# Loads that convert to bf16 on the GpSimd queue, and relu and cos/sin factor in one VectorE instruction per chunk and factor, in a cosformer attention and hypermixer kernel

## The chip, the cores and the metric

One core of one Trainium2 chip runs the whole kernel. The metric is the device time of one execution in microseconds (us), lower is better. "Fast" and "slow" after a time are the states that each execution was given: slow here means over 1.5% above the fastest execution of the same kernel in the same set. Ratios are computed from fast executions alone: the mean time of one kernel's fast runs over that of the other's of the same rounds, so not quite the ratio of the medians that I quote. A range in brackets after a ratio is its 95% interval.

TensorE (PE) does matmuls and transposes, VectorE (DVE) and ScalarE (ACT) elementwise work and the copies out of PSUM ("evictions"), GpSimd (POOL) a few memsets, SyncE (SP) issues transfers. PEld is TensorE's weight load.

## The reference, cut to what matters

```python
# q, k, v: (8 batches, 8 heads, 576, 64) fp32
theta = np.pi / 2.0 * pos / S
def phi(x, c, s):
    r = np.maximum(x, 0.0)
    return np.concatenate([r * c, r * s], axis=-1)
q_p, k_p = phi(q, cos_w, sin_w), phi(k, cos_w, sin_w)
kv  = einsum('bhsf,bhsd->bhfd', k_p, v);  z = sum(k_p, axis=2)
x   = einsum('bhsf,bhfd->bhsd', q_p, kv) / (einsum('bhsf,bhf->bhs', q_p, z) + 1e-06)
# heads side by side: x is (8, 576, 512); then the hypermixer
wq, wk = x @ w_q, x @ w_k
mixed  = (wq @ wk.T / 8) @ x
out    = relu(mixed) @ w_out
```

## The kernel before

The factor table and a weight cast that stands in VectorE's queue behind it:

```python
    inp = ctx.enter_context(tc.tile_pool(name="inp", bufs=2))
    outpool = ctx.enter_context(tc.tile_pool(name="outpool", bufs=4))
    ...
    nc.scalar.activation(cos_t, u_f, AF.Sin, bias=0.0, scale=1.0)     # [128, 9, 1] fp32
    nc.scalar.activation(sin_t, s_f, AF.Sin, bias=0.0, scale=coef)
    cossin = consts.tile([P, C9, 2, D], BF16)
    nc.vector.tensor_copy(cossin[:, :, 0, :], cos_t.to_broadcast([P, C9, D]))
    nc.vector.tensor_copy(cossin[:, :, 1, :], sin_t.to_broadcast([P, C9, D]))
    ...
    nc.vector.tensor_copy(wo_sb, wo_f)
```

Loads, relu and products. A batch is cut into `nsplit` pieces of head pairs (4 in the first batch, 2 later), so a "half-tile" below is one piece of q or k; it has 9 chunks of 64 columns per pair:

```python
    def attention(b, x_sb, nsplit):
        qf = inp.tile([P, NPAIR, C9 * D], FP32, name="qf")            # kf, vf alike
        rq = work.tile([P, NPAIR, C9, D], BF16, name="rq")            # rk alike
        q_p = work.tile([P, NPAIR, C9, 2, D], BF16, name="q_p")       # k_p alike
        ...
        for sp in range(nsplit):
            a, bb = sp * step, (sp + 1) * step
            csb = cossin.unsqueeze(1).to_broadcast([P, step, C9, 2, D])
            for dst, rr, pp, src in ((kf, rk, k_p, k), (vf, None, None, v), (qf, rq, q_p, q)):
                ...
                nc.sync.dma_start(dst[:, a:bb, :], s4[:, a:bb, :])
                if rr is None:
                    nc.any.tensor_copy(v_ext[:, a:bb, :, 0:D], ...)
                    nc.gpsimd.memset(v_ext[:, a:bb, :, D:D + 1], 1.0)
                else:
                    nc.any.tensor_scalar(rr[:, a:bb, :, :], dst[:, a:bb, :], 0.0, None, op0=ALU.max)
                    nc.vector.tensor_mul(pp[:, a:bb, :, :, :],
                        rr[:, a:bb, :, :].unsqueeze(3).to_broadcast([P, step, C9, 2, D]), csb)
```

TensorE's use of the products, one pair at a time, and the output block after every second batch:

```python
        for pr in range(NPAIR):
            for hh in range(2):
                for c in range(C9):
                    nc.tensor.matmul(kv_ps, k_p[p0:p0 + 64, pr, c, :, :], v_ext[...], ...)
                nc.any.tensor_copy(kv_sb[:, hh, :], kv_ps)            # high priority
                if hh == 0:
                    for c in range(C9):
                        nc.tensor.transpose(qpt_ps[:, c, :], q_p[:, pr, c, :, :], ident)
            nc.vector.tensor_copy(qpt_sb, qpt_ps...)                  # high priority
            ... # num_ps matmuls, reciprocal, x_sb
    def wout(b0, mix_sb):
        for rt in range(2 * S // P):
            ... # 4 matmuls into o_ps, a tile of tag "moe_ps_e"
            o_sb = outpool.tile([P, DM], FP32, name="o_sb")
            nc.any.tensor_copy(o_sb, o_ps)
            ... # two nc.sync.dma_start of o_sb to the output
```

## Time and profile before

| kernel before | |
|---|---|
| median of 3 runs | 202.64 us (201.63 to 207.41) |
| span of the profiled execution, granted clock | 206.3 us, 0.934 |
| TensorE, VectorE, ScalarE, GpSimd busy | 168.7, 136.7, 101.0, 2.7 us |

A line of groups reads: source line, engine, operation, output<-input, shapes, count | busy us, mean ns of one | idle time just before them, and what ended it. Two rows of the page that the prediction does not show matter later: the granted TensorE clock in tenths in 40 slices of the span, and the hardware queue that carries loads and stores (packets, MB, share of 16 DMA engines' time).

```profile
PEclk9999999999999999999755999999999999965896
...
q1 hardware_dynamic: 18912, 37.76, 58.1%
...
L136 PE MATMUL kv_ps<-v_ext,k_p 64*128 64x65 bf16 x576 | 38.5, 211 | 18.9 <-DVE k_p L123 16.3
...
L147 PE MATMUL qpt_ps<-ident,q_p 128*128 128x128 bf16 x288 | 31.8, 254 | 0.2 <-DVE qpt_sb L151 0.2
```

Nearly all of the wait of TensorE for products is one piece, 16.3 us at the start. Afterwards the nine kv matmuls and nine transposes of a pair find their inputs ready and run back to back.

### The profile page before, as it was taken

How to read it: one execution, taken by the hardware profiler on the slowest of the kernel's cores; microseconds unless marked ns; L12 is line 12 of the kernel's file. 1: busy time of each engine (PE TensorE's matmuls, PEld its weight loads, DVE VectorE, ACT ScalarE, POOL GpSimd, SP SyncE). 2: the span in 40 equal slices, each digit the busy share in tenths (PEclk: the TensorE clock that was granted, in tenths of full speed). 3: DMA queues.
4: the chain of work that ended last, by engine and by line, in shares of the span. 5: the costliest groups of instructions: out<-in, count | busy, mean ns of one | idle time of the engine just before them, and what ended most of it. 6: DMA issues, size and time to landing. Idle time of an engine off the chain costs nothing.

```text
span 206.3 us, 4215 instructions
## 1 busy us (share of the span) xinstructions
PE 168.7 (82%) x1696; PEld 102.8 (50%) x1696; DVE 136.7 (66%) x301; ACT 101.0 (49%) x190; POOL 2.7 (1%) x25
## 2 busy tenths in 40 slices
PE   0007889899789999999979999999799999778950
PEld 0006677555445534866645555766554575532420
DVE  1269667945877468978886898878989497723000
ACT  2174579063923645525834858239645434114540
POOL 2000000000000000000000000000000000000000
PEclk9999999999999999999755999999999999965896
DMA  6999999999500028789995066891003870000486
GB/s 189 381 358 332 401 391 391 389 341 327 198 0 2 0 54 201 165 257 394 394 391 216 0 153 147 189 362 72 3 0 80 204 180 2 3 0 0 105 204 149
DMA packets 20514, 39.32 MB, mean 191 GB/s; under 512 B 3088, under 2 KB 3088, under 8 KB 20496
## 3 DMA queue, kind: packets, MB, share of 16 engines
q1 hardware_dynamic: 18912, 37.76, 58.1%
q10 hardware_dynamic: 1584, 1.31, 2.0%
q8 instruction: 13, 0.21, 0.5%
q14 instruction: 5, 0.04, 0.1%
HBM read 29.62 MB, written 9.44 MB: 189 GB/s over the span
## 4 chain that ended last, share of the span: by engine, by line
PE 67%; DVE 10%; DMA 9%; ACT 7%; issue 2%; SPq 1%; POOL 0%; ACTq 0%; DVEq 0%
PE moe_ps_e L244 14%; PE kv_ps L136 12%; PE qpt_ps L147 11%; PE num_ps L159 7%; PE xT_ps L180 6%; DMA kf<-in_k_dram 6%; PE moe_ps_c L213 6%; PE moe_ps_a L191 6%; PE moe_ps_d L226 4%; DMA wq_f<-in_moe_w_q_dram 2%; DVE x_sb L168 2%; ACT mix_sb L233 2%; DVE qpt_sb L151 1%; DVE xT_sb L185 1%; DVE k_p L123 1%
## 5 line engine op out<-in xcount | busy, mean ns | idle before, releaser
L136 PE MATMUL kv_ps<-v_ext,k_p 64*128 64x65 bf16 x576 | 38.5, 211 | 18.9 <-DVE k_p L123 16.3
L136 PEld LDWEIGHTS <-k_p 64*128 64x128 bf16 x576 | 27.7, 106 | 29.1 <-DVE k_p L123 16.3
L244 PE MATMUL moe_ps_e<-wo_sb,mix_sb 128*128 128x512 bf16 x144 | 35.9, 410 | 0.4 <-ACT o_sb L252 0.3
L147 PE MATMUL qpt_ps<-ident,q_p 128*128 128x128 bf16 x288 | 31.8, 254 | 0.2 <-DVE qpt_sb L151 0.2
L168 DVE TENSOR_TENSOR x_sb<-num_ps,rec 128x320 bf16<-128x320 f32 x64 | 30.1, 482 | 0.1
L151 DVE COPY qpt_sb<-qpt_ps 128x1152 bf16<-128x1152 bf16 x32 | 24.2, 756 | 7.0 <-PE qpt_ps L147 6.6
L144 ACT CAST kv_sb<-kv_ps 128x65 bf16<-128x65 f32 x44 | 9.5, 216 | 36.4 <-PE kv_ps L136 35.7
L159 PE MATMUL num_ps<-kv_sb,qpt_sb 128*128 128x65 bf16 x320 | 24.0, 214 | 1.8 <-DVE x_sb L168 1.4
L252 ACT COPY o_sb<-moe_ps_e 128x512 f32<-128x512 f32 x31 | 18.2, 586 | 14.5 <-PE moe_ps_e L244 9.5
L244 PEld LDWEIGHTS <-mix_sb 128*128 128x128 bf16 x144 | 14.7, 104 | 19.1 <-issue 5.6
L147 PEld LDWEIGHTS <-q_p 128*128 128x128 bf16 x288 | 21.1, 113 | 4.1 <-issue 1.7
L180 PE MATMUL xT_ps<-ident,x_sb 128*128 128x128 bf16 (+1 forms) x160 | 19.5, 243 | 4.2 <-DVE x_sb L168 4.2
L121 ACT ACTIVATE rk<-kf 128x1152 bf16<-128x1152 f32 (+1 forms) x17 | 18.4, 1081 | 7.5 <-DMA kf<-in_k_dram 5.7
L123 DVE TENSOR_TENSOR k_p<-rk,cossin 128x2304 bf16<-128x2304 bf16 (+1 forms) x18 | 21.8, 1213 | 0.0
L123 DVE TENSOR_TENSOR q_p<-rq,cossin 128x2304 bf16<-128x2304 bf16 (+1 forms) x18 | 21.8, 1212 | 0.0
L159 PEld LDWEIGHTS <-qpt_sb 128*128 128x128 bf16 x320 | 16.9, 109 | 9.4 <-issue 3.1
L233 ACT ACTIVATE mix_sb<-moe_ps_d 128x64 bf16<-128x64 f32 (+1 forms) x40 | 14.7, 409 | 9.7 <-PE moe_ps_d L226 8.8
L121 ACT ACTIVATE rq<-qf 128x1152 bf16<-128x1152 f32 (+1 forms) x17 | 18.5, 1086 | 1.7 <-DMA qf<-in_q_dram 1.7
L226 PE MATMUL moe_ps_d<-wqkT_sb,kx_sb 64*128 64x512 bf16 x64 | 16.7, 341 | 2.4 <-ACT mix_sb L233 1.5
L233 DVE TENSOR_SCALAR mix_sb<-moe_ps_d 128x512 bf16<-128x512 f32 (+1 forms) x24 | 11.2, 475 | 10.0 <-PE moe_ps_d L226 9.7
L116 ACT CAST v_ext<-vf 128x1152 bf16<-128x1152 f32 (+1 forms) x16 | 17.5, 1103 | 0.0
L180 PEld LDWEIGHTS <-x_sb 128*128 128x128 bf16 (+1 forms) x160 | 12.2, 108 | 10.4 <-DVE x_sb L168 4.7
(40 smaller groups left out, 106.1 us busy)
## 6 DMA issues: line engine op xcount, KB each, us to landing
out_dram<-o_sb SPq DMA_DIRECT2D x72, 128.0 KB, 2.3
kf<-in_k_dram SPq DMA_DIRECT2D x14, 576.0 KB, 10.0
vf<-in_v_dram SPq DMA_DIRECT2D x14, 576.0 KB, 9.4
qf<-in_q_dram SPq DMA_DIRECT2D x14, 576.0 KB, 9.6
kf<-in_k_dram SPq DMA_DIRECT2D x4, 288.0 KB, 5.1
vf<-in_v_dram SPq DMA_DIRECT2D x4, 288.0 KB, 5.7
qf<-in_q_dram SPq DMA_DIRECT2D x4, 288.0 KB, 6.0
wo_f<-in_moe_w_out_dram ACTq DMA_DIRECT2D x1, 1024.0 KB, 9.9
```

The lines of the kernel that those rows point to most:

```text
L121: nc.any.tensor_scalar(rr[:, a:bb, :, :], dst[:, a:bb, :], 0.0, None, op0=ALU.max)
L123: nc.vector.tensor_mul(pp[:, a:bb, :, :, :], rr[:, a:bb, :, :].unsqueeze(3).to_broadcast([P, step, C9, 2, D]), csb)
L136: nc.tensor.matmul(kv_ps, k_p[p0:p0 + 64, pr, c, :, :], v_ext[p0:p0 + 64, pr, c, :], start=(c == 0), stop=(c == C9 - 1),)
L147: nc.tensor.transpose(qpt_ps[:, c, :], q_p[:, pr, c, :, :], ident)
L151: nc.vector.tensor_copy(qpt_sb, qpt_ps.rearrange("f c (hh pp) -> f hh c pp", hh=2))
L159: nc.tensor.matmul(num_ps[:, u, :], qpt_sb[:, hh, cb:cb + 2, :], kv_sb[:, hh, :], start=True, stop=True,)
L168: nc.vector.tensor_tensor(x_sb[:, :, h, :], num_ps[:, :, 0:D], rec.to_broadcast([P, SC, D]), op=ALU.mult,)
L180: nc.tensor.transpose(xT_ps[:, j0:j0 + npn], x_sb[p0:p0 + npn, u, 2 * hp:2 * hp + 2, :], ident[p0:p0 + npn, p0:p0 + npn],)
L226: nc.tensor.matmul(mx_ps[:, 0:nn], kx_sb[:, dmc * P:(dmc + 1) * P], wqkT_sb[0:64, n0:n0 + nn], start=True, stop=True,)
L233: nc.any.tensor_scalar(mix_sb[:, dmc, half * S + n0: half * S + n0 + nn], mx_ps[:, 0:nn], scale_moe, 0.0, op0=ALU.mult, op1=ALU.max,)
L244: nc.tensor.matmul(o_ps, mix_sb[:, dmc, rt * P:(rt + 1) * P], wo_sb[:, dmc, :], start=(dmc == 0), stop=(dmc == NDM - 1),)
L252: nc.any.tensor_copy(o_sb, o_ps)
```

## The change

The intent: halve what the loads write on chip, drop the relu pass and the broadcast table, and use an operation of a higher element rate.

```diff
-    inp = ctx.enter_context(tc.tile_pool(name="inp", bufs=2))
+    inp = ctx.enter_context(tc.tile_pool(name="inp", bufs=3))
...
-    cossin = consts.tile([P, C9, 2, D], BF16)
-    nc.vector.tensor_copy(cossin[:, :, 0, :], cos_t.to_broadcast([P, C9, D]))
-    nc.vector.tensor_copy(cossin[:, :, 1, :], sin_t.to_broadcast([P, C9, D]))
...
-        qf = inp.tile([P, NPAIR, C9 * D], FP32, name="qf")      # kf, vf alike; rq, rk go
+        qb = inp.tile([P, NPAIR, C9, D], BF16, name="qb")       # kb, vb alike
...
-                nc.sync.dma_start(dst[:, a:bb, :], s4[:, a:bb, :])
+                nc.gpsimd.dma_start(
+                    dst[:, a:bb, :, :].rearrange("p pr c d -> p pr (c d)"),
+                    s4[:, a:bb, :])
...
-                    nc.any.tensor_scalar(rr[:, a:bb, :, :], dst[:, a:bb, :],
-                                         0.0, None, op0=ALU.max)
-                    nc.vector.tensor_mul(
-                        pp[:, a:bb, :, :, :],
-                        rr[:, a:bb, :, :].unsqueeze(3).to_broadcast(
-                            [P, step, C9, 2, D]),
-                        csb)
+                    for c in range(C9):
+                        for w, tab in enumerate((cos_t, sin_t)):
+                            nc.vector.tensor_scalar(
+                                pp[:, a:bb, c, w, :], dst[:, a:bb, c, :],
+                                0.0, tab[:, c, :],
+                                op0=ALU.max, op1=ALU.mult)
```

More of the change, by code (lines that the diff above doesn't have):

```diff
@@ L96, in attention @@
     def attention(b, x_sb, nsplit):
-        qf = inp.tile([P, NPAIR, C9 * D], FP32, name="qf")
-        kf = inp.tile([P, NPAIR, C9 * D], FP32, name="kf")
-        vf = inp.tile([P, NPAIR, C9 * D], FP32, name="vf")
-        rq = work.tile([P, NPAIR, C9, D], BF16, name="rq")
-        rk = work.tile([P, NPAIR, C9, D], BF16, name="rk")
+        qb = inp.tile([P, NPAIR, C9, D], BF16, name="qb")
+        kb = inp.tile([P, NPAIR, C9, D], BF16, name="kb")
+        vb = inp.tile([P, NPAIR, C9, D], BF16, name="vb")
         q_p = work.tile([P, NPAIR, C9, 2, D], BF16, name="q_p")
@@ L108, in attention @@
             a, bb = sp * step, (sp + 1) * step
-            csb = cossin.unsqueeze(1).to_broadcast([P, step, C9, 2, D])
-            for dst, rr, pp, src in ((kf, rk, k_p, k), (vf, None, None, v),
-                                     (qf, rq, q_p, q)):
+            for dst, pp, src in ((kb, k_p, k), (vb, None, v), (qb, q_p, q)):
                 s4 = src[b].flatten().rearrange(
                     "(pr p e) -> p pr e", pr=NPAIR, p=P)
-                nc.sync.dma_start(dst[:, a:bb, :], s4[:, a:bb, :])
-                if rr is None:
+                nc.gpsimd.dma_start(
+                    dst[:, a:bb, :, :].rearrange("p pr c d -> p pr (c d)"),
+                    s4[:, a:bb, :])
+                if pp is None:
                     nc.any.tensor_copy(
-                        v_ext[:, a:bb, :, 0:D],
-                        dst[:, a:bb, :].rearrange("p pr (c d) -> p pr c d", c=C9))
+                        v_ext[:, a:bb, :, 0:D], dst[:, a:bb, :, :])
                     nc.gpsimd.memset(v_ext[:, a:bb, :, D:D + 1], 1.0)
                 else:
-                    nc.any.tensor_scalar(rr[:, a:bb, :, :], dst[:, a:bb, :],
-                                         0.0, None, op0=ALU.max)
-                    nc.vector.tensor_mul(
-                        pp[:, a:bb, :, :, :],
-                        rr[:, a:bb, :, :].unsqueeze(3).to_broadcast(
-                            [P, step, C9, 2, D]),
-                        csb)
+                    for c in range(C9):
[4 more added lines that the diff above has]
+                                op0=ALU.max, op1=ALU.mult)
         for pr in range(NPAIR):
```

## The prediction

> **What bounds the kernel now.** I read the busy totals, then the chain that ended last, the timeline of the start, the groups by shape, and last the pace of equal TensorE groups early and late. The totals and the chain's shares from the page:
>
> ```profile
> PE 168.7 (82%) x1696; PEld 102.8 (50%) x1696; DVE 136.7 (66%) x301; ACT 101.0 (49%) x190; POOL 2.7 (1%) x25
> ...
> PE 67%; DVE 10%; DMA 9%; ACT 7%; issue 2%; SPq 1%; POOL 0%; ACTq 0%; DVEq 0%
> ```
>
> TensorE is the bound, VectorE second. Of the 206.3 us span TensorE is idle 206.3 - 168.7 = 37.6 us. The timeline of the start shows where the largest piece lies:
>
> ```profile
> 4.72 0.46 DVE L121 TENSOR_SCALAR rk<-kf 128x576 bf16<-128x576 f32 x1
> 9.12 0.68 ACT L121 ACTIVATE rk<-kf 128x576 bf16<-128x576 f32 x1 [5.51 <-DMA kf<-in_k_dram]
> 11.69 1.23 DVE L90 CAST wo_sb<-wo_f 128x2048 bf16<-128x2048 f32 x1 [0.30 <-DMA wo_f<-in_moe_w_out_dram]
> 12.83 0.17 DVE L62 CAST r_f<-r_i 128x9 f32<-128x9 int32 x1
> 13.05 1.28 ACT L73 ACT_TABLE_LOAD   x1
> 14.34 0.21 ACT L73 ACTIVATE cos_t<-u_f 128x9 f32<-128x9 f32 x1
> 14.58 0.49 DVE L76 CAST cossin<-cos_t 128x576 bf16<-128x576 f32 x1 [0.97 <-ACT cos_t L73]
> 15.50 0.76 DVE L123 TENSOR_TENSOR k_p<-rk,cossin 128x1152 bf16<-128x1152 bf16 x1
> 16.18 0.75 DVE L123 TENSOR_TENSOR q_p<-rq,cossin 128x1152 bf16<-128x1152 bf16 x1
> 16.85 0.75 DVE L123 TENSOR_TENSOR k_p<-rk,cossin 128x1152 bf16<-128x1152 bf16 x1
> ```
>
> The first k has landed by 4.72, yet TensorE starts at 16.32: the table computation stands in VectorE's in-order queue behind the cast of wo_sb, which waits for wo_f until 11.69, and cos_t in ScalarE's queue behind relus that wait for data. So 16.3 us of the idle time is the start; some 6 us is the last eviction and store; about 15.5 us is scattered. The groups that the change touches, and two that it leaves:
>
> ```profile
> L168 DVE TENSOR_TENSOR x_sb<-num_ps,rec 128x320 bf16<-128x320 f32 x64 | 30.1, 482 | 0.1
> L151 DVE COPY qpt_sb<-qpt_ps 128x1152 bf16<-128x1152 bf16 x32 | 24.2, 756 | 7.0 <-PE qpt_ps L147 6.6
> L123 DVE TENSOR_TENSOR k_p<-rk,cossin 128x2304 bf16<-128x2304 bf16 x14 | 18.8, 1345 | 0.0
> L123 DVE TENSOR_TENSOR q_p<-rq,cossin 128x2304 bf16<-128x2304 bf16 x14 | 18.8, 1343 | 0.0
> L121 ACT ACTIVATE rq<-qf 128x1152 bf16<-128x1152 f32 x14 | 16.4, 1172 | 0.0
> L121 ACT ACTIVATE rk<-kf 128x1152 bf16<-128x1152 f32 x14 | 16.4, 1168 | 1.8 <-DVE k_p L123 1.8
> ```
>
> The products cost VectorE, the second-busiest engine; the relus cost ScalarE, which is half idle. The last piece is from the chain in order of time:
>
> ```profile
> 20.33 1.07 PE qpt_ps L147 x9
> ...
> 84.39 0.50 PE qpt_ps L147 x9
> ```
>
> The same nine transposes take 1.07 us early and 0.50 us later. By the windows, TensorE is slow from 16 to about 76 us, again around 103 to 115 and in 183 to 193 (moe_ps_c takes 2.4 us there and 1.31 us elsewhere). It becomes fast inside the dense output-matmul block.
>
> **What the Trainium skill says.** (1) "VectorE: DVE Perf Modes", section "The perf-mode tier table": tensor_tensor in bf16 tops out at two elements a cycle, tensor_scalar at four. The first half agrees: 2304 elements go in 1.27 us start to start (38.30 to 39.57), 1152 in 0.67 us; the difference is 1152 elements in 0.60 us, two a cycle, and leaves a fixed 0.07 us per instruction. No tensor_scalar of before is bf16 to bf16 with a scalar per partition, so four is not shown. (2) "SBUF — State Buffer", section "Who interferes with whom": a VectorE instruction in a two-port mode and a GpSimd instruction exclude each other for their whole length. Tensor_scalar can be in such a mode, tensor_tensor can't, and descriptors for GpSimd-queue loads are made on GpSimd. Before has no such load, so nothing here shows it. (3) "DMA: Bandwidth & Descriptors", section "Latency and other measured facts": first byte about 1 us on the GpSimd path, about 0.6 us on the hardware path. Not shown before either. (4) "TensorE: Matmul & The Clock Gate", Part 1: TensorE runs at half rate until it has been busy for a sustained stretch. The factor agrees (1.07 against 0.50); the delay does not, as 60 us of 85 to 90% busy left it slow.
>
> **The change part by part.** *Products.* Removed from VectorE: 28 x 1.27 + 8 x 0.67 = 40.9 us. Added: each half-tile becomes 9 chunks x 2 factors = 18 instructions, so 28 x 18 = 504 of 128 elements and 8 x 18 = 144 of 64. At four a cycle (0.96 GHz, the skill's clock, which the slope above confirms) and 0.07 us fixed, they take 0.103 and 0.087 us: an estimate of 51.9 + 12.5 = 64.4 us. So VectorE gets 23.5 us more work, because the fixed cost is paid 648 times instead of 36. It loses the cossin copies (0.9), two relus (0.8) and two v casts (1.4): net +20. In steady state that is 0.58 us per half-tile, 2.3 us per batch.
>
> *Relu and casts.* ScalarE loses 28 x 1.17 + 6 x 0.68 = 36.9 us, 101 to about 64. That alone is off the chain, but operations free to go to either engine (24 evictions of mix_sb, 20 of kv_sb, 5 of o_sb; about 19 us on VectorE by their groups) can move over. I take half, -10. VectorE: 136.7 + 20 - 10 = 147.
>
> *Loads.* Bytes read from memory are unchanged (28.3 MB); on-chip writes halve. Before, loads run at some 390 GB/s for the first 50 us and then pause, so their rate isn't the bound. What changes is who makes descriptors: 54 loads on GpSimd, behind its memsets of v_ext, which wait for buffers. With three input buffers I expect prefetch still to be early enough. If each load holds the shared port for 1 us (the skill's first-byte figure, used as an estimate) and half meet the new VectorE instructions, VectorE loses 27 us; I count half, 13: VectorE about 160.
>
> *Start.* No relu, no cossin copies, and wo_f meets less competition. I expect TensorE to start at about 11 us instead of 16.3: a gain of 5. But then VectorE paces the first batch: per pair 36 x 0.087 = 3.1 us of products plus 1.7 us of evictions (0.67 qpt, 0.8 x_sb, 0.2 rec), against some 3.0 us of TensorE per pair (0.61 + 1.07 + 0.61 + 0.73 from the chain). Over four pairs 1.8 x 4 = 7 us, of which before has its own part (1.34 + 1.7 is 3.0, balanced).
>
> *Sum.* TensorE busy unchanged at 168.7; start 11; end 6; scattered idle time up from 15.5 to 15.5 + 7 (first batch) + 6 (VectorE at about 75% instead of 66%, on seven batches with 2.3 us more each, a third exposed) = 28.5. Span 168.7 + 11 + 6 + 28.5 = 214; the timed median of before lies 3.7 us below its profiled span (202.64 against 206.3), so about 211 us.
>
> **Rivals.** *A: the start wins.* If cos_t is ready by 6 us and the short instructions let urgent evictions slip in between (a 1.27 us product now stands ahead of them), the start gains 9 us and the rest loses little: about 196 us. For it: the 11 us between first data and first matmul. Against: VectorE is 84% busy in the window from 15 to 25 us. *B: VectorE becomes the bound.* If the scalar per partition keeps the instruction at one element a cycle (0.203 and 0.137 us), the products are 504 x 0.203 + 144 x 0.137 = 122 us, VectorE gets about 205 us and the time is 230 or more. A full port exclusion gives something similar, 220. Against: nothing in the skill bars the mode for a scalar operand. *C: clock state.* TensorE is slow for about 80 us here. More gaps from VectorE could keep it slow longer; a full warm span less would cost 15 us, an earlier warm-up gain as much. Nothing in the profile lets me sign it. *D: hidden anyway.* If products are always made ahead, only the start and noise remain: 198 to 204.
>
> **Range and chances.** The sum gives 211. A and D pull down to 196, B and C up to 230. I take 197 to 229 as the 8-in-10 range. Faster by over 2% (below 198.6) needs A or a luckier clock: 0.20. Within 2% is D or my sum at half its size: 0.22. Slower by over 2% is my sum, B and the contention: 0.58.
>
> **What would show it.** Right: 648 tensor_scalar instructions started about 0.10 us apart; VectorE's busy share up, ScalarE's near 64 us; TensorE starting near 11 us and waiting more for k_p and q_p afterwards. Spacing near 0.20 us proves B's first form; spacing that stretches only while loads are issued proves its second. Wrong would be: start below 8 us with no new waits (A), the early nine-transpose groups at 0.5 us (C, favourable), or TensorE waiting for the loads themselves, which I gave no weight.

## The result, and the profile after

| | before | after |
|---|---|---|
| median of 4 runs | 203.03 us (201.63 to 207.41) | 279.43 us (275.34 to 282.77) |
| ratio of fast runs | | 1.3653 [1.3527, 1.378] |
| profiled execution: span, clock | 206.3 us, 0.934 | 273.5 us, 0.795 |
| TensorE busy, idle (span less busy) | 168.7, 37.6 us | 211.4, 62.1 us |
| VectorE, ScalarE, GpSimd busy | 136.7, 101.0, 2.7 us | 186.9, 79.7, 39.4 us |

The four runs after were 275.34 and 277.57 us (fast) and 281.29 and 282.77 us (slow); the profiled one is the fastest. The page of the changed kernel, the rows that answer to those of before: busy us (share of the span) and instructions of each engine, the clock, the queues, the chain that ended last by engine, and two TensorE groups:

```profile
PE 211.4 (77%) x1696; PEld 118.9 (43%) x1696; DVE 186.9 (68%) x882; ACT 79.7 (29%) x182; POOL 39.4 (14%) x79
...
PEclk9999999999999956555555999955559979555597
...
q0 software_dynamic: 13152, 14.16, 32.7%
...
PE 55%; DVE 27%; DMA 8%; ACT 4%; issue 2%; SPq 1%; ACTq 0%; DVEq 0%
...
L128 PE MATMUL kv_ps<-v_ext,k_p 64*128 64x65 bf16 x576 | 54.9, 224 | 24.3 <-DVE k_p L116 15.7
...
L139 PE MATMUL qpt_ps<-ident,q_p 128*128 128x128 bf16 x288 | 46.0, 273 | 4.8 <-DVE qpt_sb L143 3.4
```

VectorE's share of the chain rose from 10% to 27%, and its busy time by 50 us. The same 576 kv matmuls keep TensorE busy 16.4 us longer and the same 288 transposes 14.2 us longer. The clock row has more slices at 5. VectorE's groups of one shape show what was added:

```profile
L116 DVE TENSOR_SCALAR q_p<-qb,cos_t 128x128 bf16<-128x128 bf16 x126 | 31.7, 261 | 0.0
...
L116 DVE TENSOR_SCALAR k_p<-kb,cos_t 128x64 bf16<-128x64 bf16 x36 | 8.8, 260 | 0.0
```

Twice the elements take no longer each: these instructions are nearly all fixed cost. The mean of 261 ns overlaps with the next one's start, so the cost in a row of them has to be read start to start. From the timeline (start us, duration us, engine, line, operation), first those of 64 elements per partition in the first batch, then those of 128 in a later batch, while GpSimd issues loads:

```profile
20.93 0.23 DVE L116 TENSOR_SCALAR q_p<-qb,sin_t 128x64 bf16<-128x64 bf16 x1
21.08 0.23 DVE L116 TENSOR_SCALAR q_p<-qb,cos_t 128x64 bf16<-128x64 bf16 x1
...
151.59 1.40 POOL L106 DMA_DIRECT2D kb<-in_k_dram  x2 [21.64 <-DVE k_p L116]
151.69 0.25 DVE L116 TENSOR_SCALAR q_p<-qb,sin_t 128x128 bf16<-128x128 bf16 x1
151.85 0.43 DVE L116 TENSOR_SCALAR q_p<-qb,cos_t 128x128 bf16<-128x128 bf16 x1
152.01 0.30 DVE L116 TENSOR_SCALAR q_p<-qb,sin_t 128x128 bf16<-128x128 bf16 x1
```

Over longer rows they start 0.146 and 0.163 us apart, and 0.16 also here, inside the 1.40 us in which GpSimd issues two loads (151.69, 151.85, 152.01); two of them last longer there (0.43, 0.30), but the next still starts on time. Over the whole trace, the mean from one such start to the next is 162 ns outside load issues (393 gaps) and 163 inside (48). So the products take 504 x 0.163 + 144 x 0.146 = 103.2 us, where 40.9 were removed: 62.3 us more VectorE work, against 23.5 predicted.

What that does to TensorE shows in two stretches of equal length early in the run (columns: the stretch, its length, then busy us of PE, PEld, DVE, ACT and POOL with instruction counts, the clock, the DMA share, GB/s), of before and of after:

```profile
22.00:32.00 10.00, 8.59 (x106) 7.11 (x105) 6.91 (x15) 6.52 (x12) 0.26 (x2) 1.00 1.05 392
```

```profile
22.00:32.00 10.00, 6.80 (x42) 3.38 (x39) 9.68 (x60) 1.80 (x4) 3.52 (x5) 1.00 1.21 206
```

In this stretch VectorE is saturated, and TensorE gets through 42 matmuls in place of 106. It takes the chunks as they come: its first group of nine kv matmuls is cut into pieces of four, three and two with waits for k_p between them. The timeline has the first piece, and after it stand pieces of the chain (start us, us, what):

```profile
12.41 0.75 PE L128 MATMUL kv_ps<-v_ext,k_p 64*128 64x65 bf16 x4 [12.41 <-DVE k_p L116]
```

```profile
11.54 2.78 DVE k_p L116 x18
24.48 2.34 DVE k_p L116 x16
...
89.76 6.58 DMA out_dram<-o_sb
...
153.35 6.17 DMA out_dram<-o_sb
```

Two things are new in this chain: long runs of products, and two output stores of over 6 us in the middle of the run (before, the chain held one store, the last, of 2.35 us).

The saturated stretch is not where most of the time is lost. Each batch has one group of five moe_ps_c matmuls. The first of them starts at 47.97 us against 44.73 before, so after one batch the change, whose TensorE had started 3.9 us earlier, is only 3.2 us behind; the last starts at 250.54 against 183.67, 66.9 us behind. That is some 9 us in each of the seven later batches, and from 42 to 252 us VectorE is busy for 153.8 of 210 us (73%). There it is not full. It waits as well, above all for the transposes (24.7 us in all, in before 6.6):

```profile
DVE qpt_sb L143 <- PE qpt_ps L139: 24.7, 23, 2.6
```

So the two engines wait for each other in turn: TensorE for products and evictions, VectorE for the transposes that follow from the products.

### The profile page after: what moved, and what is told of

It reads as the page before. It is cut to its first block, busy times and chain, and to the rows that moved or that the text cites. A ratio compares the mean times of both kernels' runs of the same rounds, so it can differ in the third digit from the quotient of the medians.

```text
span 273.5 us, 4807 instructions
## 1 busy us (share of the span) xinstructions
PE 211.4 (77%) x1696; PEld 118.9 (43%) x1696; DVE 186.9 (68%) x882; ACT 79.7 (29%) x182; POOL 39.4 (14%) x79
## 3 DMA queue, kind: packets, MB, share of 16 engines
q0 software_dynamic: 13152, 14.16, 32.7%
q10 hardware_dynamic: 1584, 1.31, 1.5%
## 4 chain that ended last, share of the span: by engine, by line
PE 55%; DVE 27%; DMA 8%; ACT 4%; issue 2%; SPq 1%; ACTq 0%; DVEq 0%
PE qpt_ps L139 10%; PE moe_ps_e L236 9%; PE kv_ps L128 8%; DVE q_p L116 6%; PE moe_ps_c L205 6%; DVE qpt_sb L143 6%; DMA out_dram<-o_sb 6%; PE moe_ps_a L183 5%; PE xT_ps L172 5%; PE num_ps L151 5%; DVE k_p L116 5%; PE moe_ps_d L218 5%; DVE x_sb L160 4%; DVE xT_sb L177 3%; DMA wo_f<-in_moe_w_out_dram 3%
## 5 line engine op out<-in xcount | busy, mean ns | idle before, releaser
L128 PE MATMUL kv_ps<-v_ext,k_p 64*128 64x65 bf16 x576 | 54.9, 224 | 24.3 <-DVE k_p L116 15.7
L128 PEld LDWEIGHTS <-k_p 64*128 64x128 bf16 x576 | 34.3, 110 | 43.7 <-DVE k_p L116 22.3
L139 PE MATMUL qpt_ps<-ident,q_p 128*128 128x128 bf16 x288 | 46.0, 273 | 4.8 <-DVE qpt_sb L143 3.4
L143 DVE COPY qpt_sb<-qpt_ps 128x1152 bf16<-128x1152 bf16 x32 | 24.2, 757 | 24.8 <-PE qpt_ps L139 24.7
L116 DVE TENSOR_SCALAR q_p<-qb,sin_t 128x128 bf16<-128x128 bf16 (+1 forms) x162 | 40.9, 262 | 0.0
L116 DVE TENSOR_SCALAR q_p<-qb,cos_t 128x128 bf16<-128x128 bf16 (+1 forms) x162 | 40.7, 261 | 0.0
L116 DVE TENSOR_SCALAR k_p<-kb,sin_t 128x128 bf16<-128x128 bf16 (+1 forms) x162 | 40.0, 253 | 0.1
L116 DVE TENSOR_SCALAR k_p<-kb,cos_t 128x128 bf16<-128x128 bf16 (+1 forms) x162 | 39.9, 254 | 0.0
L244 ACT COPY o_sb<-moe_ps_e 128x512 f32<-128x512 f32 x36 | 21.1, 586 | 27.4 <-PE moe_ps_e L236 13.8
L106 POOL DMA_DIRECT2D kb<-in_k_dram x18 | 13.1, 728 | 86.8 <-DVE k_p L116 79.0
L190 ACT CAST wqkT_sb<-moe_ps_a 128x512 bf16<-128x512 f32 (+1 forms) x12 | 5.1, 463 | 65.8 <-PE moe_ps_a L183 65.8
L225 ACT ACTIVATE mix_sb<-moe_ps_d 128x512 bf16<-128x512 f32 (+1 forms) x51 | 19.7, 422 | 9.5 <-PE moe_ps_d L218 7.6
```

What stands on the lines that cost most here:

```text
L116: nc.vector.tensor_scalar(pp[:, a:bb, c, w, :], dst[:, a:bb, c, :], 0.0, tab[:, c, :], op0=ALU.max, op1=ALU.mult)
L143: nc.vector.tensor_copy(qpt_sb, qpt_ps.rearrange("f c (hh pp) -> f hh c pp", hh=2))
L225: nc.any.tensor_scalar(mix_sb[:, dmc, half * S + n0: half * S + n0 + nn], mx_ps[:, 0:nn], scale_moe, 0.0, op0=ALU.mult, op1=ALU.max,)
```

## The experiments

**Theory:** the 648 products cost VectorE far more than the estimate, because of a cost per instruction, and VectorE, once near saturation, passes it on to TensorE. **Rivals:** the GpSimd loads (contention with VectorE, or late data); the clock, kept low by the gaps; the order in which the chunks come; the stores. Each kernel ran four times, in four sets (1, 2, 3 and 4 below), each set with its own runs of the kernel before on the same chip: medians 206.71, 206.53, 204.69 and 205.49 us. All results were correct except e3's.

### e1: the loads alone (set 1)

```diff
 # kernel before, with
-    ... name="inp", bufs=2          qf, kf, vf FP32      nc.sync.dma_start(dst...)
+    ... name="inp", bufs=3          qf, kf, vf BF16      nc.gpsimd.dma_start(dst...)
```

> The kernel before with only the loads changed: GpSimd-queue loads that convert to bf16, three input buffers, relu and the one broadcast product kept. Theory 1 (the many short VectorE instructions are the whole cost): within 3% of before, 197 to 209 us, with TensorE starting near 16 us or earlier. Theory 2 (the GpSimd-queue loads, their later landing or the port they share with VectorE, are a large part): 235 us or more, with TensorE waiting for loads or VectorE's products stretched beyond 1.35 us.

Measured: 205.86 us (203.18 to 209.56), ratio 0.9962 [0.975, 1.0174]. The interval is just too wide to call the two the same at 2%, but there is no sign of a loss. Converting loads with the old products cost nothing that shows.

### e2: the products alone (set 1)

```diff
 # kernel before (fp32 loads by SyncE), with
-                    nc.any.tensor_scalar(rr[...], dst[...], 0.0, None, op0=ALU.max)
-                    nc.vector.tensor_mul(...)
+                    nc.any.tensor_copy(rr[...], dst[...])      # to bf16 only
+                    # then the 18 tensor_scalar of the change, reading rr; cossin removed
```

> The kernel before with only the products changed: fp32 loads on the sync queue, a plain cast to bf16 in place of the relu, then the same 648 tensor_scalar instructions as the changed kernel. Theory 1: 265 to 290 us, like the changed kernel, instructions 0.163 us apart (128 elements) and 0.146 us (64). Theory 2: 200 to 225 us, and instructions closer together[...].

Measured: 284.26 us (277.53 fast; 282.28, 286.25, 286.99 slow); no ratio of fast runs came of it. Its one fast run stands beside 275.34 and 277.57 of the changed kernel, its slow ones beside 281.29 and 282.77. In its groups by shape the 126 products of q with cos take 31.1 us, against 31.7 in the changed kernel, and in its timeline the starts are as far apart (0.162 us on the mean, and 0.146 for 64 elements), although GpSimd is busy for only 2.7 us in all here. So e1 and e2 together put the loss on the products, and rule out contention with load issuing as its cause.

### e3: a constant in place of the factor (set 1, wrong result)

```diff
 # changed kernel, with
-                                0.0, tab[:, c, :],
+                                0.0, 0.5,
```

> The changed kernel with the constant 0.5 in place of the cos or sin value per partition; wrong result on purpose, same count, shapes and dependences. If reading a scalar per partition is what made the fixed cost 0.13 us instead of the 0.07 us predicted: instructions of 128 elements 0.10 us apart, VectorE about 39 us less busy, time 225 to 255 us. If the fixed cost belongs to any such instruction: still 0.163 us apart and 270 us or more.

Measured: 232.95 us (227.29 and 230.66 fast; 235.23 and 236.63 slow), ratio 1.1178 [1.0893, 1.1462]; the result is off by 0.256, as it must be. In the timeline 18 instructions now form one line:

```profile
77.53 1.96 DVE L116 TENSOR_SCALAR k_p<-kb 128x128 bf16<-128x128 bf16 x18
79.41 1.92 DVE L116 TENSOR_SCALAR q_p<-qb 128x128 bf16<-128x128 bf16 x18
```

Eighteen take 1.88 us from start to start, and the second eighteen 1.84 (the next start is at 81.25): 0.104 and 0.102 us each; those of 64 elements 0.086 us. These are the 0.103 and 0.087 us of the prediction. So the prediction's cost was right for a constant, and a scalar per partition adds 0.060 us to every instruction: 648 x 0.060 = 39 us. VectorE's busy time fell from 186.9 to 150.0 us, by 37. The time fell by 47 us (means of fast runs, 276.5 to 229.0, from different sets). But even with the predicted instruction cost it is 229, not 211. Part of that is a wait that the prediction did not have: ScalarE waits 16.9 us for output stores in e3 (e11 and e12 show what this costs).

### e4: half as many, twice as large (set 1)

```diff
 # changed kernel, with
-        attention(b, x_sb, 4 if b == 0 else 2)
+        attention(b, x_sb, 2 if b == 0 else 1)
```

> The changed kernel with each batch in one piece (the first in two): 324 instructions of 256 or 128 elements instead of 648 of 128 or 64, the same elements. With 0.13 us fixed and four elements a cycle they are 0.197 and 0.163 us apart: 252 x 0.197 + 72 x 0.163 = 61 us in place of 103. Theory 1: 225 to 250 us. If it isn't the volume of VectorE work but the fine order or the loads: 265 us or more.

Measured: 228.80 us (228.10, 228.59, 229.02 fast; 240.88 slow), ratio 1.1158 [1.1013, 1.1303]. The timeline:

```profile
67.91 0.28 DVE L116 TENSOR_SCALAR k_p<-kb,sin_t 128x256 bf16<-128x256 bf16 x1
68.11 0.28 DVE L116 TENSOR_SCALAR k_p<-kb,cos_t 128x256 bf16<-128x256 bf16 x1
```

The spacing is 0.195 us (over a third one that starts at 68.30). Across 64, 128 and 256 elements per partition it is 0.146, 0.163 and 0.195: 128 more elements cost 0.032 us, 4.0 elements per ns, about twice the 1.9 per ns that the prediction reads from the old product (1152 in 0.60 us). The faster mode is there. What remains at zero elements is 0.13 us, paid 648 times in the change and 324 times here. VectorE's busy time is 148.3 us, as in e3, and the time is the same as e3's fast runs. Two quite different ways of taking some 37 us off VectorE give the same time.

### e5 and e6: the old kernel with VectorE work added (set 2)

Kernel before, with part of the product written a second time (e5), or all of it twice and part a third time (e6), so that the products take about 62 us (e5) or the change's 103 us (e6). Result and data flow stay as they were.

```diff
                     nc.vector.tensor_mul(pp[...], rr[...].unsqueeze(3).to_broadcast(...), csb)
+                    nc.vector.tensor_mul(pp[...], rr[...].unsqueeze(3).to_broadcast(...), csb)   # e6 only
+                    nc.vector.tensor_mul(pp[:, a:bb, :, 0, :], rr[:, a:bb, :, :], csb[:, :, :, 0, :])
```

> The kernel before with its product made one and a half times (the cosine half written again): products of about 28 x 1.94 + 8 x 1.01 = 62 us in place of 41, close to the 61 to 65 us of the half-count and constant-factor runs, but in long instructions. If VectorE's volume alone sets the time: 220 to 235 us, like those two runs (229 and 233). If the fine cutting and its order add to it: 203 to 215 us.

> The kernel before with its product made two and a half times: 28 x 3.21 + 8 x 1.68 = 103 us of products, the same as the changed kernel's 648 instructions (82 + 21 us), in 108 instructions. If VectorE's volume alone sets the time: 265 to 290 us. If the count or the fine cutting matters beyond the volume: below 250 us.

Measured: e5 223.03 us (216.38 fast; 219.95, 226.10, 226.36 slow; no ratio of fast runs), VectorE busy 154.1 us. e6 259.79 us (256.72, 257.14 fast; 262.43, 262.69 slow), ratio 1.2494 [1.2336, 1.2652]. The page of e6:

```profile
PE 191.5 (73%) x1684; PEld 113.0 (43%) x1696; DVE 187.4 (72%) x348; ACT 110.8 (43%) x215; POOL 2.7 (1%) x25
```

VectorE is as busy as in the changed kernel (186.9) in 348 instructions in place of 882. So the volume of VectorE work alone, with the old loads and the old large instructions, costs 24.9 of the 36.5 points. The exposure is high: by fast runs (before: 205.65 us on the mean) e6 lost 51 us for 62 us of added products, some 0.8; e5's one fast run lost 11 us for 21, about half. The prediction had assumed a third.

### e7 and e8: a warm TensorE from the start (set 2)

Before (e7) or the changed kernel (e8) with 64 or 46 matmuls of 512 columns on a tile of constants, issued first, while TensorE has nothing to do.

```diff
+    warm_in = consts.tile([P, 512], BF16)
+    nc.gpsimd.memset(warm_in, 0.5)
+    with tc.high_priority(100000):
+        warm_ps = psum.tile([P, 512], FP32, name="warm_ps", tag="moe", bufs=3)
+        for i in range(64):          # 46 in e8
+            nc.tensor.matmul(warm_ps, warm_in[:, 0:128], warm_in, start=True, stop=True)
```

> The kernel before with 64 extra matmuls of 512 columns on constant data at the start, in the time in which TensorE is idle (their result is not used). If TensorE's slow state of the first 70 us only needs one dense stretch to end and then lasts through the attention work: nine transposes take 0.50 us from the start and the time falls to 175 to 190 us. If attention work can't hold the fast state: 198 to 208 us, slow again within some 10 us.

> The changed kernel with 46 such matmuls at the start. If the slow clock is only inherited from the cold start: 240 to 255 us, TensorE fast for most of the span. If VectorE's starving of TensorE makes it slow: 270 to 285 us, with the clock back at half within 10 us of the first products.

Measured: e7 198.06 us (197.70, 197.87, 198.25 fast; 210.90 slow), ratio 0.9626 [0.9532, 0.9719]; e8 278.60 us (278.37 to 279.47, all fast), ratio 1.3562 [1.3429, 1.3694]. TensorE's timeline in e7, after the warm matmuls, which run from 1.46 to 17.5 us:

```profile
17.86 0.68 PE L155 MATMUL qpt_ps<-ident,q_p 128*128 128x128 bf16 x9
23.22 0.65 PE L144 MATMUL kv_ps<-v_ext,k_p 64*128 64x65 bf16 x9 [4.68 <-DVE kv_sb L152]
...
25.16 1.14 PE L155 MATMUL qpt_ps<-ident,q_p 128*128 128x128 bf16 x9
```

The first transposes run fast (0.68 us for nine; before 1.14 at the same place), then after a gap of 4.68 us they are slow again. The clock is full from about 54 us to 180 us, where before it was so only from about 76 us and with a slow stretch between 100 and 114. That is worth 3.7%, and e7 beats both kernels. In the changed kernel the same opening gives nothing: in the windows of e8 the mean clock is 0.80 from 12 to 22 us and half in the next 10 us.

```profile
22.00:32.00 10.00, 6.99 (x41) 3.45 (x38) 9.73 (x59) 1.62 (x4) 3.51 (x5) 0.50 1.21 206
```

VectorE is busy for over 97% of the stretch (9.73 of 10 us), as without the warm start (9.68): while VectorE paces, a faster TensorE gains nothing. So in these early stretches the clock is not the cause of the loss. Whether the change's products are what takes the clock away is not shown: the kernel before loses it there too (e7 at 23 us, e10 at 24). What share of the loss later in the run goes through the clock, this does not tell.

### e9: the factor outer, the chunk inner (set 3)

```diff
-                    for c in range(C9):
-                        for w, tab in enumerate((cos_t, sin_t)):
+                    for w, tab in enumerate((cos_t, sin_t)):
+                        for c in range(C9):
```

> The changed kernel with its two loops swapped: all nine cosine chunks of a half-tile, then all nine sine chunks; the same 648 instructions of the same sizes. A kv matmul needs both halves of its chunk, so TensorE is now fed in a burst near the end of each half-tile and not chunk by chunk. If the 19 us by which the changed kernel is slower than the same volume in long instructions (279 against 260) come from TensorE working chunk by chunk at VectorE's pace: 255 to 267 us, with the kv and qpt matmuls' busy time falling from 54.9 and 46.0 us towards 39 and 35. If they come from the number of instructions itself: 272 to 285 us.

Measured: 285.35 us (271.77 fast; 285.12, 285.58, 287.04 slow), no ratio of fast runs. Now all nine chunks of a half-tile become complete only at the end, so TensorE does not follow chunk by chunk: its kv group fell from 54.9 to 50.0 us busy and its transposes from 46.0 to 41.1. The time did not fall: its slow runs lie above the changed kernel's slow ones (281.29, 282.77), its fast one 5 us below the mean of the changed kernel's fast ones. The order of the chunks is not what costs most of the time, though with one fast run, between the two ranges that had been expected, a few us either way can't be told.

### e10: warm matmuls issued later, before (set 3)

Kernel before with 24 matmuls of 512 columns on `wqk_sb` right after it is written, so that they end closer to the first products.

```diff
     nc.vector.tensor_copy(wqk_sb[:, :, 1, :], wk_f)
+    with tc.high_priority(100000):
+        warm_ps = psum.tile([P, 512], FP32, name="warm_ps", tag="moe", bufs=3)
+        warm_in = wqk_sb.rearrange("p c w j -> p (c w j)")
+        for i in range(24):
+            nc.tensor.matmul(warm_ps, warm_in[:, 0:128], warm_in, start=True, stop=True)
```

> The kernel before with 24 dense matmuls on the projection weights instead of 64 on a constant: they start when the weights are cast (about 6 us) and end near 14 us, and with 24 of them VectorE's order at the start stays as before, with the first eviction after four products and not after nine. If the stall of 4.7 us (kv_ps waiting for the eviction) is what took the clock back in the 64-matmul run: the clock stays full from the start, 180 to 192 us. If the attention work itself can't hold it: 195 to 205 us, slow again between about 20 and 55 us.

Measured: 200.07 us (199.54, 199.95, 200.19 fast; 203.42 slow), ratio 0.9811 [0.9743, 0.9879]. Less than e7. In windows of its TensorE work alone (the stretch, its length, PE busy, clock, DMA share, GB/s) the clock is lost in the middle of steady work (0.73 on the mean of the 3 us between the two), where the longest gap before a TensorE instruction was 0.73 us:

```profile
20.00:23.00 3.00, 2.28 (x48) 1.00 1.03 386
...
26.00:29.00 3.00, 2.73 (x32) 0.50 1.05 389
```

### e11 and e12: twelve output buffers (set 4)

The changed kernel (e11), and e4 (e12), each with:

```diff
-    outpool = ctx.enter_context(tc.tile_pool(name="outpool", bufs=4))
+    outpool = ctx.enter_context(tc.tile_pool(name="outpool", bufs=12))
```

The reason for the run is in the timeline of the changed kernel's ScalarE, around the first of the long stores, and in its list of waits (engine, tile, line, what it waited for: us in all, times, longest):

```profile
96.50 0.58 ACT L244 COPY o_sb<-moe_ps_e 128x512 f32<-128x512 f32 x1 [3.18 <-DMA out_dram<-o_sb]
```

```profile
ACT o_sb L244 <- DMA out_dram<-o_sb: 13.5, 10, 3.2
```

Before, the same kind of wait came to 4.9 us, 0.8 at the longest. ScalarE wants a free output buffer and waits for a store.

> The changed kernel with 12 output buffers in place of 4; TensorE's, VectorE's and GpSimd's instructions stand in the same order. In the changed kernel's chain two stores of 6.58 and 6.17 us stand (2.4 is usual): the eviction of the output waits for a buffer whose store runs beside casting loads. If this collision makes up most of the 19 us between 279 and the 260 us of the same VectorE volume in long instructions: 262 to 270 us. If it is hidden by VectorE's delay anyway: 274 to 282 us.

> The half-count version (229 us, three stores of some 6.2 us in its chain) with 12 output buffers. If the collision sets its end: 211 to 221 us, below the 223 us of the same product time in long instructions. If not: 225 to 232 us.

Measured: e11 269.85 us (269.52 to 271.76, all fast), ratio 1.3331 [1.3186, 1.3475]; e12 218.21 us (216.85, 217.41, 219.00 fast; 222.21 slow), ratio 1.075 [1.0524, 1.0976]. The order of instructions on TensorE, VectorE and GpSimd is the same in e11 as in the changed kernel; the wait of ScalarE for stores is gone and no store but the last is in the chain. So the stores were worth 3.2 points in the changed kernel (1.3653 to 1.3331) and 4.1 in e4 (1.1158 to 1.075), some 6 to 8 us; in both pairs the intervals do not overlap, and every fast run lies below every fast run of the other. TensorE's largest wait in e11:

```profile
PE kv_ps L128 <- DVE k_p L116: 14.4, 7, 11.7
```

This and the next two, 7.9 and 7.8 us for x_sb, are all for VectorE, as in the changed kernel (15.7, 8.0 and 7.8 us).

### Where the 36.5% are

Added VectorE volume costs 24.9 points (e6) and the stores 3.2 (e11 against the changed kernel). The remaining 8.4, some 17 us, lie between e6 and e11, and stay open. They are not in TensorE's idle time (69.1 us in e6, 55.8 in e11: span less busy) but in its busy time: 191.5 us in e6, 214.2 in e11. The kv matmuls and transposes, 74.7 us in e6, take 100.7 in e11 (100.9 in the changed kernel). Two causes could do that, a slow clock for longer and small pieces issued as chunks come. The traces speak against the clock. The kv matmuls of e6, then of e11 (between the bars: busy us, mean ns of one):

```profile
L145 PE MATMUL kv_ps<-v_ext,k_p 64*128 64x65 bf16 x576 | 39.3, 219 | 32.6 <-DVE k_p L133 23.1 <-ACT kv_sb L153 7.7 <-DVE kv_sb L153 1.7
```

```profile
L128 PE MATMUL kv_ps<-v_ext,k_p 64*128 64x65 bf16 x576 | 54.6, 222 | 20.9 <-DVE k_p L116 14.4 <-ACT kv_sb L136 2.4 <-DVE qpt_sb L143 1.3
```

One matmul takes as long in both (one transpose too, 277 and 274 ns), but fewer of them overlap, so the group's busy time is longer: waiting for VectorE chunk by chunk is counted as busy. That this costs the time is not shown, since e9, which feeds TensorE in bursts, is not clearly faster. VectorE's wait for the transposes grows as well, from 17.0 us in e6 to 24.6 in e11, and this mutual waiting may be the 17 us; no run isolates it. At half the count (e12, 7.5%) the volume alone (e5, whose one fast run lies 5% above the fast runs of before) leaves little to explain.

## Why the prediction was wrong

The direction was right: slower by over 2% had 0.58. The time, 211 us with a range up to 229, was far too low. By its steps:

- **Products: the mis-sized term.** "0.07 us fixed ... an estimate of 51.9 + 12.5 = 64.4 us" measured 103.2 us. The rate of four a cycle held (0.146, 0.163 and 0.195 us for 64, 128 and 256 elements), the count held (648). The fixed cost is 0.13 us, not 0.07: the 0.07 was taken from a tensor_tensor and carried over to an instruction with a scalar per partition. e3 shows it directly, 0.103 us with a constant as predicted and 0.163 with the scalar. This is 39 us of VectorE, and 47 us of time (e3 against the changed kernel). The Trainium skill had a hint that the prediction left out: "VectorE: DVE Perf Modes", the section on the TRN2 errata, puts a fixed cost on every such instruction, 58 cycles of 0.96 GHz, and advises tiles of 512 elements or more. Its formula, an estimate of 0.094 us for 128 elements at four a cycle, lies near e3's 0.103 and well below 0.163. (The section says itself that the formula falls short of what a single copy took, whose fixed part it puts at about 150 cycles.)
- **"A third exposed" was the second.** With the predicted instruction cost (e3) the time is still 229 (fast runs), of which some 8 us may be the stores (what e4 lost by them). e6 shows about 0.8 of the added VectorE work arriving in the time, e5's one fast run about half, not a third. The copies that TensorE waits for (qpt_sb, x_sb, kv_sb) stand in the same queue as the products. In the stretch from 22 to 32 us there was no VectorE idle time left to hide anything in; later there was (73% busy from 42 us on), but it lay where VectorE waited for TensorE. The mean share of 66% before was no measure of room.
- **"TensorE busy unchanged at 168.7"** measured 211.4. The count of 1696 matmuls is unchanged; two other things are not. The kv matmuls and transposes take 30.6 us more by their groups, though one of them takes only 6 to 7% longer (211 to 224 ns, 254 to 273): they come in smaller pieces and overlap less. Elsewhere it is the clock. At half clock a group of five moe_ps_c matmuls takes 2.4 us, at full clock 1.31; of the eight such groups, one for each batch, 6 were slow in the changed kernel's profile and 4 in that of before. Idle time rose as well, from 37.6 to 62.1 us; the part between first and last matmul went from 13.8 us (the prediction had taken 15.5) to 42.4, against 28.5 predicted.
- **Contention, counted as 13 us, did not happen.** The spacing stays 0.163 us while GpSimd issues loads; e1, with the same loads, is no slower than before, and e2, without them, is as slow as the changed kernel.
- **"TensorE waiting for the loads themselves, which I gave no weight":** rightly for the loads as such. But the other transfers did change: 18 of the 72 stores took over 5 us from issue to landing, where before none took over 4 (the median stays at 2.4), and waiting for them cost 6 to 8 us, which no step of the prediction had. The change of the loads is what slows them: with it alone (e1) 7 stores took over 5 us, without it (e2, e6) none. Whether it is the conversion, the other queue or the third input buffer, no run tells apart.
- **Right:** TensorE's start, 12.41 us against "about 11" (16.32 before), and the first batch paced by VectorE. ScalarE's "about 64" was 79.7: the prediction took 10 us of evictions off VectorE but did not add them to ScalarE, where mix_sb, kv_sb and o_sb rose by 10.0 us (42.4 to 52.4). The rest is overlap: its instructions add up to 111.5 us before (101.0 busy) and 85.0 after (79.7).
- **Rival B** is nearest. Its spacing (0.203) was too large, its mechanism (one element a cycle) wrong, its verdict, a time of 230 or more set by VectorE's products, right; VectorE as the one bound holds only for the start (see the batches above). Rival C is partly right as a consequence: e7 shows an earlier full clock to be worth 3.7% to the kernel before, e8 nothing to the changed one. A and D, which had the loss hidden, did not come about.

The hoped-for gain from smaller loads was not there either. The converted packets land half as large (14.16 MB in 13152 packets), but one takes 0.327 x 273.5 x 16 / 13152 = 109 ns of an engine, against 0.581 x 206.3 x 16 / 18912 = 101 ns in the queue of before. The early window says the same: the DMA share is full in both, at 206 GB/s in place of 392.

## What to carry to other kernels

Before splitting an operation to get a faster mode, measure start to start what one small instruction costs with the very operands it will have: here a scalar per partition made 0.163 us of 0.103, and 648 of them outweighed twice the element rate. On an engine that also does the evictions the main engine waits for, don't count added work as hidden because its mean share leaves room: here 62 us added to VectorE cost 51 (e6), at 72% busy. And when loads change their path, look at what else shares the DMA engines, for stores and their buffer count can become the new wait.

## What the Trainium skill lacked or had wrong

- "VectorE: DVE Perf Modes", the section on the TRN2 errata: it gives the fixed cost (58 cycles by its formula, about 150 for a single copy) without regard to the kind of scalar. The runs show that the operand matters: 0.103 us start to start for 128 bf16 elements with a constant, 0.163 with an fp32 scalar per partition (0.086 and 0.146 for 64). No page that I read gives this 0.06 us.
- "SBUF — State Buffer", section "Who interferes with whom": it says that a VectorE instruction in a two-port mode and GpSimd shut each other out. In the changed kernel no cost shows: the products start 163 ns apart inside load issues and 162 outside, and a load takes GpSimd 0.70 us to issue both there and in e1. Only e4 shows a trace of it: its instructions of 256 elements start 0.237 us apart on the mean inside load issues (14 gaps, the longest 0.348) against 0.196 outside, 0.6 us in all.
- "TensorE: Matmul & The Clock Gate", Part 1: it names about 3.4 us of sustained work as enough to become fast, and an idle window of that length as what makes TensorE slow. In e7 a dense stream became fast some 4.2 us after its start (631 ns for one matmul until then, 379 after), near what the page has. But before stayed slow through 50 us at 87 to 91% busy (16 to 66 us), for which the page gives no rule, and e10 lost the clock at about 24 us with no gap over 0.73 us since 18 us. Also, the recorded clock reads 1.00 at the start of every run although nine transposes take 1.07 us there in before, as at half clock; the durations are the safer reading.
- "DMA: Bandwidth & Descriptors": it says that a converting transfer has to go by the GpSimd queue, not what it costs. Here a packet took 109 ns for half the landed bytes, against 101 ns before, and a load took GpSimd 0.7 us to issue (1.40 us for two).
- No page that I read has the slow stores: with the converting loads 18 of 72 took over 5 us (up to 6.8), against 2.4 us for the median and none over 4 before.
